# First 512 tokens as one block, masks of the second batch on VectorE, and exponentials that wait at a table change

## The chip, the cores and the metric

The kernel runs on one core of one Trainium2 chip. The metric is the device time of one execution in microseconds; the time before is the median of three runs. A profiled execution of the same program, whose rows are read below, has a span (first to last instruction) and a time of its own. TensorE appears in the rows as PE (matrix products) and PEld (loads of the stationary operand), VectorE as DVE, ScalarE as ACT, GpSimd as POOL, SyncE as SP.

## The reference

Four batches of 576 tokens go through an attention of 8 heads of 64 columns, then through two feed-forward layers (512 to 2048 to 512). In heads 0 to 3 a token sees itself and the 31 tokens before it ("local"), in heads 4 to 7 every 32nd token before it ("strided").

```python
scores = scale * np.matmul(q, k.transpose(0, 1, 3, 2))
masks = np.stack([mask_local if h < H // 2 else mask_strided for h in range(H)], axis=0)
scores = np.where(masks[None, :, :, :], scores, -1000000000.0)
...
attn = attn / (np.sum(attn, axis=-1, keepdims=True) + 1e-09)
return np.matmul(attn, v).astype(np.float32)
# x: the 2304 tokens of attn_out, 512 columns
h = x @ w_in;  g = h * np.tanh(softplus(h));  x = g @ w_out      # first layer ("moe")
h = x @ w_in;  g = h - np.tanh(h);            return g @ w_out   # second layer ("moe2")
```

The weights of both layers arrive as 64-bit floats.

## The kernel before

**A planner writes the order.** Every piece of work is a task (class `Plan`, `add`) with a cost for each engine that can do it, a key, the tasks that it follows and the buffers that it takes and frees. While the program is built, `Plan.run` goes through the tasks by modelled time: of all waiting tasks it takes the one that can start first, and of equals the one with the smaller key, and so fixes the order of the instructions on each engine. Keys come from a list of due times (`due`), which walks over the steps below at modelled TensorE costs (`pe_cost`), with `ATTEND` added for a step that runs beside attention. A function of another table on ScalarE (`EXPS` for exp and ln, `MISH`, `TANH`) costs a table load (L193), modelled as `SWITCH`, and its key is raised by `PATIENCE`. `fill` (L479) puts small matrix products on TensorE into gaps that the planner sees early in the program.

**Attention** is done in 16 pairs of heads (`pair`), four for each batch, two strided and then two local, and each pair in two halves (`half_pair`): scores (L589), row maxima, exponentials (L634 or L645), normalisation, transposes on TensorE (L697), their copies (L449, L451), the products with v (L715), and the copy of the result to `xr`. The first batch (`BY_PE`) leaves the division to the end: the totals are summed on TensorE (L731) and ScalarE inverts them (L735, L738), VectorE multiplies (L749). In batches listed in `LEAN`, the first two, TensorE adds the mask to the scores by a bf16 product with an identity (L586), VectorE reduces to the maxima (L617), and ScalarE reads the scores out of PSUM, whose banks it frees; ScalarE may also normalise (L665). In the others VectorE adds the mask, takes the maximum and writes the masked scores to SBUF in one instruction per unit (`masked_max`, L622), which frees the banks at once.

**The first layer** runs over blocks of tokens and 16 chunks of 128 hidden columns. A step (`step`) is one chunk of one block: 12 products (`gemm1`, L855: four pieces of 128 input columns, each with high part by high, low by high, and high by low part), then on ScalarE the activation (L874), its split into parts (L449 or L451, and L455), and two steps later (`LAG`) 12 products of `gemm2` (L906). Before, the blocks are 256, 256, 512, 384, 512 and 384 tokens wide, and the first two are run against each other: five steps of the first, then one of each in turn, so that a new chunk of weights is needed every second step. Both take their x straight from the attention of the first batch (`x_split`); two local pairs (`LATE`) load and compute their second halves later, since the first block needs only tokens 0 to 255. Later blocks load x from DRAM (`x_load`). Two sets of x tiles (`TB`, 512 and 384 wide) alternate between blocks.

**Weights** (`weights`): each of the 32 half chunks is loaded, shrunk (L402 or L405), turned to fp32 by three VectorE instructions (L414, L419, L424), and split (a cast on ScalarE or VectorE, a subtraction on VectorE).

**The second layer** (`unit`, `factors`) runs over 512, 512, 512, 512 and 256 tokens with a scheme of seven products instead of eight; its weights are made from 64-bit floats (`keep_in`, `keep_out`) while the last blocks of the first layer run.

Of the kernel before, what the change touches and what calls it, by code (L numbers as in the profile page):

```python
# [56 lines left out]
class Plan:  # L57
# [15 lines left out]
    def add(self, engs, fn, key, after=(), take=(), give=(), dma=None, start=0.0, rows=128, table=None, bulk=False):  # L73
# [9 lines left out]
        return t  # L83

    WINDOW = 3.4133
    warm, window, busy, heat, table = False, 0, 0.0, 0.0, None
# [44 lines left out]
    def run(self):  # L131
# [14 lines left out]
        while left:  # L146
# [5 lines left out]
            for e, q in waiting.items():  # L152
                for t in q:
                    start = self.room(t, max(engines[e], t.ready, now))
                    if start == INF:
                        continue
                    key, end = t.key, start + t.engs[e]
                    if e == ACT and t.table not in (None, self.table):
                        key += self.PATIENCE
                        end += self.SWITCH  # L160
                    if best is not None and (start, key) >= best[:2]:
                        continue
                    if any(
                        u.key + HOLD < t.key and start < u.ready < end - 0.05
                        and end - u.ready > HOLDW * (u.ready - start) and self.room(u, u.ready) < end
                        and all(max(engines[o], u.ready) + c > u.ready + HOLDO for o, c in u.engs.items() if o != e)
                        for u in q
                    ):
# [49 lines left out]
def pe_cost(n):  # L218
    return {256: 0.12, 384: 0.174, 512: 0.227}.get(n, 0.0004375 * n + 0.007)
# [23 lines left out]
def attention_two_moe(  # L243
# [17 lines left out]
    scale = 1.0 / float(D) ** 0.5  # L261
    blocks = [[256, 256, 512, 384, 512, 384], [512] * 4 + [256]]
    TB = (512, 384)
# [13 lines left out]

    pieces2 = [(0, starts[0][2])] + list(zip(starts[0], blocks[0]))[2:]
    x2d = {
# [68 lines left out]

    steps = [(0, 0, c) for c in range(HEAD)]
    for c in range(NC):  # L350
        steps += [(0, 1, c)] + ([(0, 0, c + HEAD)] if c + HEAD < NC else [])
    steps += [(0, j, c) for j in range(2, len(blocks[0])) for c in range(NC)]
    NU, HALF = NC // 2, 256
# [4 lines left out]
    for l, j, c in steps:  # L358
        if l == 0 and j == 0:
            t_ = max(t_, FIRST + PACE * c)  # L360
        due.append(t_)
        if l == 0:
            t_ += 24 * pe_cost(blocks[l][j]) + (ATTEND if 1 < j < 5 else 0.0)
        else:
            t_ += (42 if blocks[1][j] > HALF else 24) * pe_cost(HALF) + 6 * blocks[1][j] // 128 * pe_cost(DM)
    due += [t_, t_ + 4, t_ + 8, t_ + 12]
    first_use = [min(step_of[0, j, c] for j in range(2)) for c in range(NC)]

# [119 lines left out]

    BY_PE, LEAN = (0,), (0, 1)
    ON_ACT = [(0, 0), (0, 1), (1, 0), (1, 1)]  # L490

    def pair(i):
# [274 lines left out]

        inner = starts[0][2]
        x_slot = ["xr0", "wi9", "wo9", "wi8"][i] if first else "xr0"
        xb = Buf([x_slot], 5) if first else Buf([x_slot], 1)  # L770
        done = [half_pair(0), half_pair(1)]
        plan.link(*done)
        cols = slice(inner, S) if first else slice(0, S)
        if first:
            for j in range(2):
                t0, n = starts[0][j], blocks[0][j]
                x_split(0, j, p, [done[0]] if i in LATE and j == 0 else done,
                        lambda t0=t0, n=n: st["x"][:, t0:t0 + n], xb,
                        k0 + 3 if j == 0 else due[step_of[0, 1, 0]] - 3)
            free_first[x_slot] = [split[j][p][1] for j in range(2)]  # L780
            for n, what in enumerate("qkv"):
                free_first[slot_of_first(i, what)] = last_s[i] if what != "v" else last_pv
# [28 lines left out]
    def x_load(l, j, p, key):  # L811
# [18 lines left out]

        after = [x_store[p, c[0]] if l == 0 else x2_store[p, 0, c[0] + 1] for c in cut]
        J = len(blocks[0]) * l + j
        x = add({SP: 0.45 * len(cut)}, load, key - 5, after + [last_g1[J - 2]], take=[buf], dma=0.7)
        x_split(l, j, p, [x], lambda: h["t"], buf, key)
# [6 lines left out]
    def step(s):  # L841
# [50 lines left out]
        m = KC  # L892

        both = J < 2
        wide = starts[0][2] if both else n
        cols = slice(starts[0][J], starts[0][J] + n) if both else slice(0, wide)
        opens, closes = c == 0 and J != 1, c == NC - 1 and J != 0
        k2 = due[s + LAG] + 0.1
        for f in range(m):
# [16 lines left out]
            if closes:  # L916
# [9 lines left out]
                def store(e, f=f):  # L926
                    nc.sync.dma_start(out=x2d[f, j - 1], in_=t_ev[J, f])

# [191 lines left out]
    def factors(j, key, ready):  # L1120
# [5 lines left out]
        def load_of(x):  # L1126
# [15 lines left out]

            after = [x2_store[2 * lower + k, 0, i[0] + 1] for k in range(2) for i in cut] + old
            return add({SP: 0.9 * len(cut)}, load, key - 5 + len(raw_loads), after, take=[buf], dma=0.7), buf

        def tiles():
# [8 lines left out]
            hi = [one_(t[:, 2 * i:2 * i + 2]) for t in (a, b) for i in range(m)]  # L1155
            if J % 2 == 0:
                lo = [hi.pop()] + [one_(sb([128, 2, HALF], F32R, slot, "xq")) for slot in ("q0", "q1", "k0", "k1")]
                t = sb([128, 4, HALF], F32R, "v", "xq")
                lo += [one_(t[:, :2]), one_(t[:, 2:])]
            else:  # L1160
                hi += [one_(sb([128, 2, HALF], F32R, "xr0", "xq"))]
                t = sb([128, 9, HALF], F32R, "pp", "xq")
                lo = [one_(t[:, 2 * i:2 * i + 2]) for i in range(4)]
                lo += [one_(cols(W2[u, 3][:, 1, :])) for u in (2 * NS, 2 * NS + 1)]
                lo += [two_(*(sb([128, 1, HALF], F32R, f"pT{i}", "xq") for i in range(2)))]
            xq[J] = list(zip(hi, lo))
# [248 lines left out]
    with tc.manual_schedule():  # L1415
# [8 lines left out]
        for c in range(NC):  # L1424
            for half in "io":
# [9 lines left out]
                weights(0, half, c, free_first.get(tag, []), due_w - 3.514, kd)  # L1435
        for s in range(2 * NC):
# [40 lines left out]
        order = [(i, g) for i in range(len(pairs)) for g in range(2)]  # L1477
        x, y = LATE
        order[2 * x:2 * x + 4] = [(x, 0), (y, 0), (x, 1), (y, 1)]
        for a, b in zip(order, order[1:]):  # L1480
# [56 lines left out]
```

## Time and profile before

| | |
|---|---|
| median of three runs | 892.72 us (891.67 to 892.78) |
| profiled execution | 891.31 us, span 889.5 us |
| TensorE products busy | 882.3 us (99% of the span), 6080 instructions |
| VectorE busy | 593.0 us (67%) |
| ScalarE busy | 429.3 us (48%), 89.8 us of it in 70 table loads |
| granted TensorE clock, mean | 0.999 |

A product on TensorE is shown longer than the distance to the next one, because products overlap; what one costs in a stream is read from start to start, or from the merged pieces of the chain of work. The same holds for the instructions of VectorE and ScalarE, less strongly. Idle time in square brackets stands behind the instruction that it precedes, with what ended it.

### The profile page before, as it was taken

To read this page: it belongs to the slowest core of one execution; us is meant where nothing else is said; L and a number is where in the kernel's file an instruction comes from. 1 tells how busy PE (TensorE), PEld (TensorE's weight loads), DVE (VectorE), ACT (ScalarE), POOL (GpSimd) and SP (SyncE) were. 2 spreads that over 40 slices of the span, in tenths; PEclk is the share of its full clock that TensorE was granted. 3 is DMA by queue.
4 is the path that set the end of the run, shared out by engine and by line. 5 is a ranking of instruction groups with operands and counts; after the bars stand their busy time and mean duration, and the time that the engine had idled before them with its cause. 6 is when DMAs were issued, how large, how long until landed. Compare 5 with 4: busy or idle time off the path is not lost.

```text
span 889.5 us, 16480 instructions
## 1 busy us (share of the span) xinstructions
PE 882.3 (99%) x6080; PEld 788.3 (89%) x6080; DVE 593.0 (67%) x1578; ACT 429.3 (48%) x910; POOL 2.4 (0%) x13
## 2 busy tenths in 40 slices
PE   8999999999999999999999999999999999999998
PEld 7899999877778999888999999898999889998896
DVE  6999998556565657778776885575457545555533
ACT  7999999656446625443444532252224222322211
POOL 1000000000000000000000000000000000000000
PEclk9999999999999999999999999999999999999999
DMA  9981113411112149877787443352235223655531
GB/s 308 379 340 55 59 59 102 150 62 33 63 66 91 43 149 317 253 260 258 252 282 233 133 152 102 112 190 95 96 132 176 95 96 119 209 169 162 175 125 62
DMA packets 84657, 138.19 MB, mean 155 GB/s; under 512 B 10016, under 2 KB 37152, under 8 KB 84576
## 3 DMA queue, kind: packets, MB, share of 16 engines
q1 hardware_dynamic: 84576, 137.14, 46.1%
q8 instruction: 48, 0.79, 0.4%
q14 instruction: 33, 0.27, 0.1%
HBM read 107.22 MB, written 29.88 MB: 154 GB/s over the span
## 4 chain that ended last, share of the span: by engine, by line
PE 93%; ACT 4%; DVE 1%; DMA 1%; issue 0%; SPq 0%; ACTq 0%
PE acc L1382 22%; PE h L855 22%; PE acc L906 22%; PE hx L1245 18%; PE hx L1262 3%; PE sps L589 2%; PE ops L715 2%; PE ptps L697 2%; ACT p L645 1%; DMA kT<-in_k_dram 1%; ACT stwo L402 0%; ACT pT L449 0%; ACT L193 0%; ACT stwi L402 0%; ACT dd L735 0%
## 5 line engine op out<-in xcount | busy, mean ns | idle before, releaser
L855 PE MATMUL h<-xh,wi 128*128 128x256 f32 (+2 forms) x768 | 215.1, 342 | 0.6 <-ACT B L874 0.5
L906 PE MATMUL acc<-gh,wo 128*128 128x256 f32 (+2 forms) x768 | 196.5, 341 | 0.0
L1382 PE MATMUL acc<-w,gh 128*128 128x512 f32 x576 | 179.1, 392 | 0.0
L1245 PE MATMUL hx<-xq,w 128*128 128x256 f32 x1280 | 174.1, 284 | 0.0
L1245 PEld LDWEIGHTS hx<-xq,w 128*128 128x128 f32 x1280 | 167.6, 191 | 6.5
L855 PEld LDWEIGHTS h<-xh,wi 128*128 128x128 f32 x768 | 137.9, 189 | 14.4 <-ACT B L874 1.0
L906 PEld LDWEIGHTS acc<-gh,wo 128*128 128x128 f32 x768 | 132.1, 189 | 10.4
L855 PE MATMUL h<-xl,wi 128*128 128x256 f32 (+2 forms) x384 | 129.4, 337 | 0.1
L906 PE MATMUL acc<-gl,wo 128*128 128x256 f32 (+2 forms) x384 | 128.9, 336 | 0.0
L1382 PEld LDWEIGHTS acc<-w,gh 128*128 128x128 f32 x576 | 103.2, 188 | 18.1 <-DVE gh L451 0.4
L1382 PE MATMUL acc<-w,gl 128*128 128x512 f32 x288 | 112.2, 389 | 0.0
L1333 ACT ACTIVATE th<-hx 128x256 f32<-128x256 f32 x48 | 18.5, 385 | 160.2 <-PE hx L1245 120.1
L193 ACT ACT_TABLE_LOAD x70 | 89.8, 1283 | 1.2
L874 ACT ACTIVATE B<-h 128x256 f32<-128x256 f32 (+2 forms) x96 | 46.9, 492 | 89.5 <-PE h L855 87.0
L1338 DVE SCALAR_TENSOR_TENSOR H<-hx,th 128x256 f32<-128x256 f32 x48 | 20.3, 423 | 98.7 <-ACT th L1333 98.6
L455 DVE TENSOR_TENSOR gl<-B,gh 128x256 fp32r<-128x256 f32 (+2 forms) x96 | 52.9, 553 | 46.6 <-ACT gh L449 44.1
L1333 ACT ACTIVATE th<-H 128x256 f32<-128x256 f32 x64 | 33.5, 524 | 95.2 <-PE acc L1382 51.0
L455 DVE TENSOR_TENSOR H<-H,hx 128x256 f32<-128x256 f32 x160 | 66.9, 418 | 17.3 <-PE hx L1245 8.4
L906 PEld LDWEIGHTS acc<-gl,wo 128*128 128x128 f32 x384 | 72.5, 189 | 5.1
L855 PEld LDWEIGHTS h<-xl,wi 128*128 128x128 f32 x384 | 72.5, 189 | 5.0 <-DVE xl L455 0.3
L1382 PEld LDWEIGHTS acc<-w,gl 128*128 128x128 f32 x288 | 54.1, 188 | 12.1 <-DVE gl L455 0.2
L1338 DVE SCALAR_TENSOR_TENSOR H<-H,th 128x256 f32<-128x256 f32 x64 | 35.7, 558 | 40.2 <-ACT th L1333 39.9
(118 smaller groups left out, 1020.7 us busy)
## 6 DMA issues: line engine op xcount, KB each, us to landing
w<-w2o SPq DMA_DIRECT2D x160, 256.0 KB, 2.6
stwi<-in_moe_w_in_dram SPq DMA_DIRECT2D x16, 512.0 KB, 7.7
stwo<-in_moe_w_out_dram SPq DMA_DIRECT2D x16, 512.0 KB, 8.9
w2v<-in_moe_w_out_dram SPq DMA_DIRECT2D x32, 256.0 KB, 4.0
w2o<-p SPq DMA_DIRECT2D x48, 128.0 KB, 3.4
w<-w2i SPq DMA_DIRECT2D x24, 256.0 KB, 3.0
out_dram<-ev SPq DMA_DIRECT2D x18, 256.0 KB, 3.7
w2v<-in_moe_w_in_dram SPq DMA_DIRECT2D x8, 512.0 KB, 3.9
```

Source lines behind the costliest of these rows:

```text
L193: self.load_table(t.table)
L455: eng.tensor_tensor(out=out, in0=a, in1=b, op=op)
L589: nc.tensor.matmul(s[a][:, at_, :], tq[64 * a:64 * a + 64, q0:q0 + nq], tk[64 * a:64 * a + 64, k0_:k0_ + nk], start=not lean, stop=not lea ...
L697: nc.tensor.transpose(t[:, n, :], h["p", a][:, n, :], ident[:nq, :nq])
L855: nc.tensor.matmul(h_ps[s], w[:, wp, kc, :], xx[:, kc, :n], start=(kc == first_kc and i == 0), stop=(kc == last_kc and i == 2),)
L874: nc.scalar.activation(out=b_tile(), in_=h_ps[s], func=ACTF.Mish, scale=2.0 ** -8)
L906: nc.tensor.matmul(acc[f][:, cols], w[:, wp, 128 * f:128 * f + 128], g, start=(opens and i == 0), stop=(closes and i == 2),)
L1245: nc.tensor.matmul(st[t], w[:, wp, 256 * i + 128 * k:256 * i + 128 * k + 128], unit_of(xq[J][x][xp], k)[:, 0], start=(q in (1, 6, 7, 5) an ...
L1262: nc.tensor.matmul(st[t], w[:, wp], unit_of(xq[J][kc // 2][xp], kc % 2)[:, 0], start=(kc == 0 and m == 0), stop=(kc == KC - 1 and m == 2),)
L1333: nc.scalar.activation(out=st["th", i][:, cols], in_=x, func=ACTF.Tanh, scale=2.0 ** -8)
L1338: nc.vector.scalar_tensor_tensor(out=st["H", i][:, cols], in0=x, scalar=2.0 ** -8, in1=st["th", i][:, cols], op0=ALU.mult, op1=ALU.subtract,)
L1382: nc.tensor.matmul(acc[f], g[:, 128 * f:128 * f + 128], where[wp](), start=(opens and m == 0), stop=(closes and m == 2),)
```

## The change

The first two blocks become one of 512 tokens, and the widths are 512, 384, 512, 384, 512; no pair is late, all four pairs of the first batch are loaded and computed whole before the first step ends. The tiles of the second layer's x swap their places to follow the new count of blocks. `LEAN` loses the second batch: its masks and maxima are those of the third and fourth, and its normalisation is VectorE's alone. In the planner a task of the exp table that needs a table load may start no earlier than 6.0 us after it became ready; tasks of the table that is loaded are free of this.

```diff
+    DWELL = {EXPS: 6.0}
...
                     if e == ACT and t.table not in (None, self.table):
                         key += self.PATIENCE
-                        end += self.SWITCH
+
+                        start = max(start, t.ready + self.DWELL.get(t.table, 0.0))
+                        end = start + t.engs[e] + self.SWITCH
...
-    blocks = [[256, 256, 512, 384, 512, 384], [512] * 4 + [256]]
+    blocks = [[512, 384, 512, 384, 512], [512] * 4 + [256]]
...
-    steps = [(0, 0, c) for c in range(HEAD)]
-    for c in range(NC):
-        steps += [(0, 1, c)] + ([(0, 0, c + HEAD)] if c + HEAD < NC else [])
-    steps += [(0, j, c) for j in range(2, len(blocks[0])) for c in range(NC)]
+    steps = [(0, j, c) for j in range(len(blocks[0])) for c in range(NC)]
...
-            t_ += 24 * pe_cost(blocks[l][j]) + (ATTEND if 1 < j < 5 else 0.0)
+            t_ += 24 * pe_cost(blocks[l][j]) + (ATTEND if j < 4 else 0.0)
...
-        since = max(x_due[b - 1], due[step_of[0, 1, 0]])
+        since = max(x_due[b - 1], due[step_of[0, 0, 1]])
...
-    LATE = (2, 3)
-    pass
+    LATE = ()
...
-    BY_PE, LEAN = (0,), (0, 1)
+    BY_PE, LEAN = (0,), (0,)
...
         if first:
-            for j in range(2):
-                t0, n = starts[0][j], blocks[0][j]
-                x_split(0, j, p, [done[0]] if i in LATE and j == 0 else done,
-                        lambda t0=t0, n=n: st["x"][:, t0:t0 + n], xb,
-                        k0 + 3 if j == 0 else due[step_of[0, 1, 0]] - 3)
+            n = blocks[0][0]
+            x_split(0, 0, p, done, lambda: st["x"][:, :n], xb, k0 + 3)
...
-            if J % 2 == 0:
-                lo = [hi.pop()] + [one_(sb([128, 2, HALF], F32R, slot, "xq")) for slot in ("q0", "q1", "k0", "k1")]
+            if J % 2 == 1:
+                lo = [one_(sb([128, 2, HALF], F32R, slot, "xq")) for slot in ("q0", "q1", "k0", "k1", "xr0")]
...
-        for J in range(2, last + 1):
-            if J < 2 + B - 1:
-                for i in range(KC * (J - 1), KC * J):
+        for J in range(1, last + 1):
+            if J < B:
+                for i in range(KC * J, KC * J + KC):
                     pair(i)
```

## Rows read from the trace of the kernel before

**Rows 1.** Busy time by engine in three stretches; PEclk is the granted clock.
```profile
38.48:60.00 21.52, 20.99 (x198) 18.88 (x197) 21.48 (x52) 21.39 (x50) 0.00 (x0) 1.00 1.02 399
60.00:155.00 95.00, 94.96 (x949) 89.06 (x949) 89.39 (x282) 92.39 (x231) 0.00 (x0) 1.00 0.25 78
155.00:320.00 165.00, 165.00 (x1124) 137.53 (x1119) 96.69 (x390) 92.66 (x133) 0.00 (x0) 1.00 0.23 74
```

**Rows 2.** Order of time on PE, 30 to 157 us: start, length, work.
```profile
30.12 0.36 PE L855 MATMUL h<-xh,wi 128*128 128x256 f32 x1
...
32.89 0.39 PE L855 MATMUL h<-xl,wi 128*128 128x256 f32 x1
...
38.36 0.28 PE L855 MATMUL h<-xh,wi 128*128 128x256 f32 x1
...
43.88 0.71 PE L731 MATMUL tot<-pT,ones 128*64 128x288 f32 x4
...
45.14 0.47 PE L697 MATMUL ptps<-ident,p 96*128 96x96 f32 x3
...
58.67 0.38 PE L855 MATMUL h<-xh,wi 128*128 128x256 f32 x1 [0.53 <-ACT B L874]
...
156.59 0.48 PE L855 MATMUL h<-xh,wi 128*128 128x512 f32 x1
```

**Rows 3.** Chain that ended last, merged pieces: start, length, work.
```profile
85.75 1.44 PE h L855 x12
...
355.47 2.72 PE acc L906 x12
...
501.86 5.08 PE hx L1245 x42
```

**Rows 4.** Order of time on PE around scores, with and without mask products.
```profile
52.80 0.41 PE L586 MATMUL sps<-mstrb,identb 72*72 72x288 bf16 x2
53.14 0.74 PE L589 MATMUL sps<-kT,qT 64*72 64x72 f32 x16
...
93.88 0.49 PE L586 MATMUL sps<-mfirst,identb 96*96 96x384 bf16 x2
94.30 0.90 PE L589 MATMUL sps<-kT,qT 64*96 64x128 f32 x12
...
274.40 0.39 PE L906 MATMUL acc<-gl,wo 128*128 128x512 f32 x1
274.72 0.90 PE L589 MATMUL sps<-kT,qT 64*96 64x128 f32 x12
```

**Rows 5.** Order of time on DVE: results of the first batch's half pairs.
```profile
13.97 0.68 DVE L749 TENSOR_TENSOR xr<-ops,dd 128x288 f32<-128x288 f32 x1 [0.53 <-ACT dd L738]
...
30.86 0.44 DVE L749 TENSOR_TENSOR xr<-ops,dd 128x288 f32<-128x288 f32 x1
...
46.40 0.45 DVE L749 TENSOR_TENSOR xr<-ops,dd 128x288 f32<-128x288 f32 x1
...
52.39 0.45 DVE L749 TENSOR_TENSOR xr<-ops,dd 128x288 f32<-128x288 f32 x1
```

**Rows 6.** Order of time on DVE: maxima with TensorE's mask, then with VectorE's.
```profile
63.43 0.81 DVE L617 TENSOR_REDUCE rows<-sps 72x4 f32<-72x288 f32 x2
...
134.25 0.23 DVE L622 CUSTOM_DVE_ANT_0 p<-sps,mstr 72x72 f32<-72x72 f32 x1 [0.42 <-PE sps L589]
...
135.47 0.45 DVE L455 TENSOR_TENSOR p<-p,rows 72x288 f32<-72x288 f32 x1
```

**Rows 7.** Groups on ACT, 36 to 150 us: count, busy us, mean ns.
```profile
L193 ACT ACT_TABLE_LOAD x34 | 43.6, 1283 | 0.6
...
L665 ACT ACTIVATE p<-p,rows 96x128 f32<-96x128 f32 x12 | 3.8, 398 | 0.0
L665 ACT ACTIVATE p<-p,rows 72x72 f32<-72x72 f32 x8 | 2.2, 355 | 0.0
```

**Rows 8.** Order of time on ACT: last result of the second batch.
```profile
138.53 0.39 ACT L449 ACTIVATE xr<-ops 128x288 f32<-128x288 f32 x1
```

More of the change, by code (lines that the diff above doesn't have):

```diff
@@ L276, in attention_two_moe @@
     starts = [[sum(bl[:j]) for j in range(len(bl))] for bl in blocks]
-    pieces2 = [(0, starts[0][2])] + list(zip(starts[0], blocks[0]))[2:]
+    pieces2 = list(zip(starts[0], blocks[0]))
     x2d = {
@@ L366, in attention_two_moe @@
     due += [t_, t_ + 4, t_ + 8, t_ + 12]
-    first_use = [min(step_of[0, j, c] for j in range(2)) for c in range(NC)]
+    first_use = [step_of[0, 0, c] for c in range(NC)]
     def block_of(token):
@@ L766, in pair @@
         last_pv = []
-        inner = starts[0][2]
+        inner = starts[0][1]
         x_slot = ["xr0", "wi9", "wo9", "wi8"][i] if first else "xr0"
-        xb = Buf([x_slot], 5) if first else Buf([x_slot], 1)
+        xb = Buf([x_slot], 3) if first else Buf([x_slot], 1)
         done = [half_pair(0), half_pair(1)]
@@ L774, in pair @@
         if first:
-            for j in range(2):
-                t0, n = starts[0][j], blocks[0][j]
-                x_split(0, j, p, [done[0]] if i in LATE and j == 0 else done,
-                        lambda t0=t0, n=n: st["x"][:, t0:t0 + n], xb,
-                        k0 + 3 if j == 0 else due[step_of[0, 1, 0]] - 3)
-            free_first[x_slot] = [split[j][p][1] for j in range(2)]
-            for n, what in enumerate("qkv"):
+            n = blocks[0][0]
+            x_split(0, 0, p, done, lambda: st["x"][:, :n], xb, k0 + 3)
+            free_first[x_slot] = [split[0][p][1]]
+            for n_, what in enumerate("qkv"):
                 free_first[slot_of_first(i, what)] = last_s[i] if what != "v" else last_pv
@@ L829, in load @@
                 nc.sync.dma_start(out=t[:, lo - t0:hi - t0], in_=src[:, lo - a:hi - a])
-        after = [x_store[p, c[0]] if l == 0 else x2_store[p, 0, c[0] + 1] for c in cut]
+        after = [x_store[p, c[0]] if l == 0 else x2_store[p, 0, c[0]] for c in cut]
         J = len(blocks[0]) * l + j
-        x = add({SP: 0.45 * len(cut)}, load, key - 5, after + [last_g1[J - 2]], take=[buf], dma=0.7)
+        x = add({SP: 0.45 * len(cut)}, load, key - 5, after + [last_g1.get(J - 2)], take=[buf], dma=0.7)
         x_split(l, j, p, [x], lambda: h["t"], buf, key)
@@ L892, in step @@
         m = KC
[L894 to L897, printed above, removed]
+        wide, cols = n, slice(0, n)
+        opens, closes = c == 0, c == NC - 1
         k2 = due[s + LAG] + 0.1
@@ L926, in store @@
                 def store(e, f=f):
-                    nc.sync.dma_start(out=x2d[f, j - 1], in_=t_ev[J, f])
+                    nc.sync.dma_start(out=x2d[f, j], in_=t_ev[J, f])
                 ev = add({ACT: act_cost(wide, True), DVE: dve_cost(wide)}, evac, k2 - 8, [x], take=[eb], give=[ab])
@@ L1141, in load @@
                         nc.sync.dma_start(out=t[:, k, lo - a0:hi - a0], in_=x2d[2 * lower + k, i][:, lo - a:hi - a])
-            after = [x2_store[2 * lower + k, 0, i[0] + 1] for k in range(2) for i in cut] + old
+            after = [x2_store[2 * lower + k, 0, i[0]] for k in range(2) for i in cut] + old
             return add({SP: 0.9 * len(cut)}, load, key - 5 + len(raw_loads), after, take=[buf], dma=0.7), buf
@@ L1155, in tiles @@
             hi = [one_(t[:, 2 * i:2 * i + 2]) for t in (a, b) for i in range(m)]
-            if J % 2 == 0:
-                lo = [hi.pop()] + [one_(sb([128, 2, HALF], F32R, slot, "xq")) for slot in ("q0", "q1", "k0", "k1")]
+            if J % 2 == 1:
+                lo = [one_(sb([128, 2, HALF], F32R, slot, "xq")) for slot in ("q0", "q1", "k0", "k1", "xr0")]
                 t = sb([128, 4, HALF], F32R, "v", "xq")
                 lo += [one_(t[:, :2]), one_(t[:, 2:])]
+                hi += [two_(*(sb([128, 1, HALF], F32R, f"pT{i}", "xq") for i in range(2)))]
             else:
-                hi += [one_(sb([128, 2, HALF], F32R, "xr0", "xq"))]
+                lo = [hi.pop()]
                 t = sb([128, 9, HALF], F32R, "pp", "xq")
-                lo = [one_(t[:, 2 * i:2 * i + 2]) for i in range(4)]
+                lo += [one_(t[:, 2 * i:2 * i + 2]) for i in range(4)]
                 lo += [one_(cols(W2[u, 3][:, 1, :])) for u in (2 * NS, 2 * NS + 1)]
-                lo += [two_(*(sb([128, 1, HALF], F32R, f"pT{i}", "xq") for i in range(2)))]
             xq[J] = list(zip(hi, lo))
@@ L1435, in attention_two_moe @@
                 weights(0, half, c, free_first.get(tag, []), due_w - 3.514, kd)
-        for s in range(2 * NC):
+        for s in range(NC):
             step(s)
         last = len(blocks[0]) - 1
-        for J in range(2, last + 1):
-            if J < 2 + B - 1:
-                for i in range(KC * (J - 1), KC * J):
+        for J in range(1, last + 1):
+            if J < B:
+                for i in range(KC * J, KC * J + KC):
                     pair(i)
@@ L1477, in attention_two_moe @@
         order = [(i, g) for i in range(len(pairs)) for g in range(2)]
-        x, y = LATE
-        order[2 * x:2 * x + 4] = [(x, 0), (y, 0), (x, 1), (y, 1)]
         for a, b in zip(order, order[1:]):
```

## The prediction

> **What bounds the kernel now.** I read the busy time by stretches first. From 60 to 155 us TensorE is busy for 94.96 of 95.00 us, from 155 to 320 for all of it, at the full granted clock [rows 1]; the page's total (99%) says the same of the rest. So after the start the end is set by the work that TensorE has to do, and a change is worth what it takes from that work, plus what it does to the moment at which TensorE starts to be fed. The second view is TensorE in order of time near 30 to 60 us: the first step begins at 30.12 in pieces, and from 38.48, 0.12 behind the last row of that start, the stream is closed but for one wait of 0.53 us on an activation [rows 2]. The third is the chain of work, from which I take what a product costs in a stream [rows 3]. VectorE and ScalarE come last: they are nearly full as well from 38 to 155 us (89.39 and 92.39 of 95) and far from it later (97 and 93 of 165) [rows 1]. They are hidden, but in the stage that the change rebuilds the cover is thin.
>
> **Wider first block.** Before, 2 blocks x 16 steps x 24 = 768 products of 256 columns: 12 take 1.44 us, 0.120 each, so 92.2 us. After, 384 of 512 columns: 12 take 2.72 us, 0.2267 each, so 87.0 us [rows 3]. That is **-5.1 us**, the largest term. The 256-column price is no effect of the crowded stage: at 501.86 us, in the second layer, 42 products of 256 columns take 5.08 us, 0.121 each [rows 3]. The Trainium skill (TensorE: Matmul & The Clock Gate, section Back-to-back issue gap) gives an isolated warm product N/2.4 + 2.5 ns. As an estimate by that page, halving the count would save 384 x 2.5 ns, about 1.0 us; the rows differ from it, and they are of this kernel. The same widths follow in another order; the rest of the layer's products are unchanged.
>
> **Masks off TensorE.** A half pair of the second batch loses two bf16 products. Their distance to the first score is 53.14 - 52.80 = 0.34 us when strided and 94.30 - 93.88 = 0.42 when local [rows 4]; four of each make 3.0 us, the upper bound. But where scores follow a layer's product with no mask between, there is a hole: 274.40 + 0.227 = 274.63, and the scores start at 274.72 [rows 4], 0.09 us that the mask covered. I take that off eight times: **-2.3 us**.
>
> **The start.** All eight half pairs of the first batch must now be done before the first step can go past its first quarter. Six results came between 13.97 and 30.86 us, one per 3.4 us [rows 5]. Two more at this pace bring the eighth to 37.6. In the trace the product that needs the low part of the sixth's x starts at 32.89, 2.0 us after its result's start [rows 2, 5]; with 512 columns to split I use that. TensorE is fed for good from 39.6 us, instead of 38.48. What it has behind it by then differs: before, 30 products of 256 (first at 30.12, last at 38.36) [rows 2], 3.6 us; after, three of 512, 0.7. And before, 4.1 us of the first batch's attention were still to come: the last scores with their mask (0.42 + 0.83), twice totals and products with v (45.14 - 43.88 = 1.26 each) and transposes (about 0.3) [rows 2, 4]; after, none. Sum: 39.6 - 38.48 + 3.6 - 0.7 - 4.1 = -0.1. Between results 3.0 and 3.9 us apart the term is -0.9 to +0.9. I take **-0.1**. The chunks are no hurdle there: a new chunk is due every 24 x 0.2267 = 5.4 us instead of 2.9 for the first five.
>
> **Work for VectorE and ScalarE.** Eight masked units take 135.47 - 134.25 = 1.22 us, two reductions 0.81 [rows 6]: 0.41 more per half pair, 3.3 us for eight taking the strided price for all. Twenty ScalarE instructions normalise six tiles now [rows 7] (three a local, four a strided tile); on VectorE each takes about 0.45 [rows 6]: 2.7 more. Fewer, wider splits give about 1.4 back (two of 256 columns against one of 512). So VectorE has some 4.6 us more to do, and the stage is 7.5 us shorter, against 95 - 89.39 = 5.6 us idle [rows 1]. I still price it at nothing: in that stage VectorE also starts on the third batch (the masked units at 134.25 are its), which can wait until after 155 us, where 40% of VectorE is idle, and it does casts and copies that ScalarE can take.
>
> **Waiting exponentials.** ScalarE loads tables 34 times from 36 to 150 us, 43.6 us [rows 7], nearly half its time. If exponentials gather for 6 us, I expect some 16 to 22 loads there and 40 to 55 in all instead of 70. No load is TensorE's wait, but for the 0.53 us, so this is worth at most **0.5 us**, which I leave out against small new waits; it frees 15 to 20 us of ScalarE and so pays for the cover above. What it delays: each half pair by up to 6 us, and behind it transposes and products with v. The clock I take as it is: the gaps of the start are filled with small products as before.
>
> **Sum.** -5.1 - 2.3 - 0.1 = -7.5 us. The profiled execution (span 889.5) had 891.31, 1.4 below the median of 892.72. Span after: 882.0; profiled time 883.8; median **885.2**. With the bounds together (-5.1 - 3.0 - 0.9 - 0.5, and -5.1 - 2.3 + 0.9) 883.2 to 886.2; since the planner writes every order anew, I call 882.2 to 888.2 this case: 0.64.
>
> **Rivals.** (1) *The start is later.* Halves seven and eight of the trace came 52.39 - 46.40 = 6.0 us apart [rows 5], when weights shared both engines. If that is the pace, TensorE is fed 2 x 2.6 = 5.2 us later: 890.4. Against it: they had low keys there, and now they have the same high keys as the first six. 0.13.
> (2) *The width saves little*, since the 13 ns by which a 256-column product exceeds half a 512 one go with weight loads and their neighbours: only the masks and the start are left, -2.4 us: 890.3. The second layer's row at 501.86 speaks against it [rows 3]. 0.04. The page of the Trainium skill cited above would have it nearly so, with 1.0 us kept.
> (3) *VectorE becomes the bound.* If ScalarE isn't relieved and the third batch can't wait (its tokens are needed from 896 instead of 1024 on, a quarter of a block sooner), VectorE lacks 4.6 + 7.5 - 5.6 = 6.5 us, which TensorE waits out: 891.7. 0.06.
> (4) *Slower: the waiting exponentials make the second batch late for the second block.* Its first scores are at 52.80 and its last result at 138.53 [rows 4, 8], 10.7 us per half pair; the first step that needs it starts at 156.59 [rows 2], 18 us later. With two half pairs in flight, w us of waiting each add up to 8w / 2, at 6 us 24. The stage gets 7.5 us shorter, so 10.5 of the lead are left: TensorE waits from w = 2.6 on, the kernel is slower from w = 4.5 on, and at 6 us it is -7.5 + 13.5 = +6.0: 898.7. Against it: at 10.7 us a half pair the pace is the planner's choice and not the chain's, and the second batch's keys now begin after the first step instead of the fifth, some 15 us earlier by the list of due times. 0.07.
> (5) *The wait does nothing*: loads stay near 70. As ScalarE is off the path, the time is that of the forecast, and it is no case of its own. The remaining 0.06 is for what I don't see, half on each side.
>
> **Numbers.** 0.2% (1.8 us) is about what a measurement of this kernel can tell from no change. Forecast, rivals 1 and 2 and half the rest are faster: 0.84. Same: rival 3 and a little, 0.08. Slower: rival 4 and a little, 0.08. The range 882.0 to 890.5 holds the forecast and rivals 1 and 2, some 0.81.
>
> **What would show it.** Right: 1152 products of 512 columns in L855 and L906 and none of 256, at 2.72 us per 12; L586 with 16 instructions, not 32; the first step's second quarter at 38 to 41 us and no gap on TensorE above 0.5 us after it; table loads well under 70; VectorE above 95% until about 145 us and the first 384-column step at 147 to 150. Wrong: the stream closing at 43 us or later; waits of TensorE on weights (VectorE) or on x of the second block; 512-column products dearer than 0.23 us beside attention.

## The result, and the profile after

The changed kernel has a median of **883.66 us** over 20 executions, the kernel before, beside it on the same chip, 892.41: ratio 0.9912, 95% interval 0.9886 to 0.9938. The forecast was 885.2, with a range of 882.0 to 890.5. In 5 of the 20 executions the mean granted clock was 0.984 to 0.987 instead of 1.0 and the time 891.3 to 894.1; the ratio takes these in (the two medians alone stand at 0.9902), the first profile is one of them, and "the profile after" is therefore that of the first experiment below, the same kernel at 884.06 us with a span of 882.3, against 891.31 and 889.5 before.

Busy time by stretches (as in [rows 1]: start and end, length, then busy us and instructions of PE, PEld, DVE, ACT, POOL, then PEclk, DMA share, GB/s):

```profile
38.48:60.00 21.52, 21.49 (x185) 17.23 (x183) 21.30 (x78) 19.29 (x50) 0.00 (x0) 1.00 1.00 391
60.00:155.00 95.00, 94.69 (x610) 73.35 (x611) 90.85 (x315) 75.38 (x177) 0.00 (x0) 1.00 0.27 90
155.00:320.00 165.00, 165.00 (x1134) 141.85 (x1133) 96.57 (x385) 75.49 (x125) 0.00 (x0) 1.00 0.24 77
```

TensorE stays full. VectorE has a little more to do from 60 to 155 us than before, ScalarE 17 us less (75.38 against 92.39).

Groups of TensorE by shape (count, busy us, mean ns):

```profile
L851 PE MATMUL h<-xh,wi 128*128 128x512 f32 x384 | 132.0, 399 | 0.0
L899 PE MATMUL acc<-gh,wo 128*128 128x512 f32 x384 | 120.4, 394 | 0.0
...
L851 PE MATMUL h<-xl,wi 128*128 128x512 f32 x192 | 75.1, 391 | 0.0
L899 PE MATMUL acc<-gl,wo 128*128 128x512 f32 x192 | 75.0, 391 | 0.0
...
L478 PE MATMUL fill<-ones 128*128 128x128 bf16 x155 | 12.6, 252 | 1.0 <-DVE ones L1412 1.0
...
L585 PE MATMUL sps<-mfirst,identb 96*96 96x384 bf16 x8 | 2.0, 326 | 0.0
L585 PE MATMUL sps<-mstrb,identb 72*72 72x288 bf16 x8 | 1.7, 293 | 0.0
```

These are the 1152 products of 512 columns that were forecast; no group of 256 columns is left in L851 and L899 (L855 and L906 before). The mask products are 16 instead of 32, the filling products 155, where the kernel before has 176.

The chain of work, merged pieces (start, length, work), answering to [rows 3]:

```profile
68.89 2.72 PE h L851 x12
71.61 2.72 PE acc L899 x12
...
120.26 0.68 DVE gl L455
...
127.42 0.60 DVE wo L455
...
132.91 0.47 PE ptps L696 x3
```

Twelve products of 512 columns cost 2.72 us beside attention too, as taken. From 120.26 to 132.91 the chain runs over VectorE: the cover was used up, though not overdrawn, for TensorE's idle time in all of 60 to 155 us is 0.31 us, the wait for VectorE's maxima that ends at 132.91.

The start, in order of time on TensorE (answers to [rows 2]):

```profile
1.00 6.13 PE L478 MATMUL fill<-ones 128*128 128x128 bf16 x57 [1.00 <-DVE ones L1412]
...
32.47 0.74 PE L588 MATMUL sps<-kT,qT 64*72 64x72 f32 x16
...
35.88 0.50 PE L851 MATMUL h<-xh,wi 128*128 128x512 f32 x1
...
39.57 0.74 PE L588 MATMUL sps<-kT,qT 64*72 64x72 f32 x16
40.25 1.29 PE L478 MATMUL fill<-ones 128*128 128x128 bf16 x20
41.35 0.48 PE L851 MATMUL h<-xh,wi 128*128 128x512 f32 x1
```

In the kernel before the first line reads:

```profile
1.00 4.79 PE L479 MATMUL fill<-ones 128*128 128x128 bf16 x57 [1.00 <-DVE ones L1419]
```

The first and the last two results of the first batch, in order of time on VectorE (answers to [rows 5]):

```profile
15.15 0.68 DVE L748 TENSOR_TENSOR xr<-ops,dd 128x288 f32<-128x288 f32 x1 [0.90 <-ACT dd L737]
...
36.10 0.45 DVE L748 TENSOR_TENSOR xr<-ops,dd 128x288 f32<-128x288 f32 x1
...
38.95 0.45 DVE L748 TENSOR_TENSOR xr<-ops,dd 128x288 f32<-128x288 f32 x1
```

The second quarter of the first step starts at 41.35 (forecast 39.6, with 38 to 41 as the sign of being right). Scores of the second batch already stand in front of it, at 32.47 and 39.57. The first step of 384 columns starts at 144.27; the forecast was 147 to 150. Groups on ScalarE, table loads in the whole span:

```profile
L196 ACT ACT_TABLE_LOAD x38 | 48.8, 1283 | 0.6
```

38 loads instead of 70; 16 of them from 36 to 150 us, where [rows 7] have 34.

### The profile page after: what moved, and what is told of

Its sections match the earlier page's. It is cut to its first block, busy times and chain, and to the rows that moved or that the text cites. A ratio compares the mean times of both kernels' runs of the same rounds, so it can differ in the third digit from the quotient of the medians.

```text
span 891.9 us, 15576 instructions
## 1 busy us (share of the span) xinstructions
PE 884.7 (99%) x5659; PEld 771.4 (86%) x5659; DVE 588.3 (66%) x1633; ACT 391.6 (44%) x851; POOL 2.4 (0%) x13
## 4 chain that ended last, share of the span: by engine, by line
PE 95%; DVE 2%; DMA 1%; ACT 1%; issue 0%; SPq 0%; DVEq 0%
PE acc L1375 22%; PE h L851 22%; PE acc L899 21%; PE hx L1238 18%; PE sps L588 3%; PE hx L1255 3%; PE ops L714 2%; PE ptps L696 2%; DMA kT<-in_k_dram 1%; PE tot L730 1%; PE fill L478 1%; DVE wcv L424 0%; DVE wcv L419 0%; PE sps L585 0%; DVE wo L455 0%
## 5 line engine op out<-in xcount | busy, mean ns | idle before, releaser
L851 PE MATMUL h<-xh,wi 128*128 128x512 f32 (+1 forms) x640 | 207.2, 377 | 0.0
L899 PE MATMUL acc<-gh,wo 128*128 128x512 f32 (+1 forms) x640 | 186.4, 372 | 0.0
L851 PEld LDWEIGHTS h<-xh,wi 128*128 128x128 f32 x640 | 119.1, 188 | 17.0 <-ACT B L870 0.2
L899 PEld LDWEIGHTS acc<-gh,wo 128*128 128x128 f32 x640 | 116.4, 188 | 15.1
L851 PE MATMUL h<-xl,wi 128*128 128x512 f32 (+1 forms) x320 | 117.9, 368 | 0.0
L899 PE MATMUL acc<-gl,wo 128*128 128x512 f32 (+1 forms) x320 | 117.8, 368 | 0.0
L870 ACT ACTIVATE B<-h 128x512 f32<-128x512 f32 (+1 forms) x80 | 44.5, 556 | 117.9 <-PE h L851 113.7
L455 DVE TENSOR_TENSOR gl<-B,gh 128x512 fp32r<-128x512 f32 (+1 forms) x80 | 50.8, 635 | 41.7 <-ACT gh L449 39.6
L899 PEld LDWEIGHTS acc<-gl,wo 128*128 128x128 f32 x320 | 60.1, 188 | 7.7
L851 PEld LDWEIGHTS h<-xl,wi 128*128 128x128 f32 x320 | 60.2, 188 | 6.4
L455 DVE TENSOR_TENSOR gl<-H,gh 128x512 fp32r<-128x512 f32 (+1 forms) x80 | 51.1, 639 | 7.5 <-ACT gh L449 4.5
```

What stands on the lines that cost most here:

```text
L455: eng.tensor_tensor(out=out, in0=a, in1=b, op=op)
L851: nc.tensor.matmul(h_ps[s], w[:, wp, kc, :], xx[:, kc, :n], start=(kc == first_kc and i == 0), stop=(kc == last_kc and i == 2),)
L870: nc.scalar.activation(out=b_tile(), in_=h_ps[s], func=ACTF.Mish, scale=2.0 ** -8)
L899: nc.tensor.matmul(acc[f][:, cols], w[:, wp, 128 * f:128 * f + 128], g, start=(opens and i == 0), stop=(closes and i == 2),)
```

## Experiments

The theory to be tested is that of the forecast: TensorE is the bound, the wider block and the masks each take their part off it and add up, and the wait of the exponentials is worth nothing. Rivals: the parts do not add (VectorE has room for the masks only if the block is wide); the wait holds up the second batch; the width saves little. A to H in the expectations are explained there; two more letters, further down, are theories on the clock: J, that TensorE's wait for keys near 8 to 10 us lets the granted clock fall, and K, that the thin stretch of 10 to 28 us does so by itself. Kernels of one group ran on one chip beside the kernel before.

**The changed kernel again**, unchanged.

> The changed kernel as it is. In 15 of its 20 executions it took 882.5 to 884.1 us at a granted clock of 0.999 to 1.000, in 5 of them 891.3 to 894.1 at 0.984 to 0.987; the profile that was kept is one of the five. Theory A (the gain is TensorE work: widths -5.1, masks -2.3, start about 0): undisturbed executions at 883 to 884.5 again, 0.990 to 0.992 of the kernel before, and in an undisturbed profile a span of 881 to 882.5 with the first step's second quarter at 38 to 41 us. Rival B (the start is earlier or later than I reckoned, and the width or mask term is off to match): the same time, but a second quarter outside 38 to 41 us.

883.45 us (12 executions), ratio 0.9929 [0.9897, 0.9962]; four of the 12 at 891.8 to 893.6. Its profile is shown above: the span of 882.3 is the expected one, the second quarter at 41.35 lies 0.35 us outside the expected 38 to 41. So, by the letter, it is rival B that came: the time is right and the terms are not quite.

**Without the wait.**

```diff
-    DWELL = {EXPS: 6.0}
+    DWELL = {}
```

> The changed kernel without the 6 us wait of exponentials. Theory A: ScalarE is off the path, so the wait is worth at most 0.5 us: 883 to 885 undisturbed, and some 65 to 75 table loads instead of the changed kernel's count. Rival C (the wait pays for the cover: without it ScalarE and VectorE are short in the first block and TensorE waits): 886 us or more, with waits of TensorE on weights or x between 45 and 150 us.

883.07 us, ratio 0.9906 [0.9870, 0.9941]; 58 table loads instead of 38 (65 to 75 were expected). The wait saves 20 loads, 26 us of ScalarE, and no time: within this change it is worth 0 to what can be measured.

**Masks of the second batch back on TensorE**, wait kept.

```diff
-    BY_PE, LEAN = (0,), (0,)
+    BY_PE, LEAN = (0,), (0, 1)
```

> The changed kernel with the second batch's masks, and its right to normalise on ScalarE, given back. Theory A: +2.3 us (3.0 at most), 885.5 to 887 undisturbed, with 16 more mask products. Rival D (VectorE has no room in that stage, so taking 5 us off it repays the 2.3): no change, 883 to 884.5. Rival E (scores that wait in PSUM for exponentials hold the banks, so giving the masks back costs more than the products): 888 or more.

895.16 us, ratio 1.0043 [1.0013, 1.0073], as rival E has it: 11.7 us more than with the masks on VectorE, five times the mask term. TensorE in order of time, the second batch's local scores and what follows:

```profile
102.27 0.90 PE L588 MATMUL sps<-kT,qT 64*96 64x128 f32 x12
...
117.42 0.90 PE L588 MATMUL sps<-kT,qT 64*96 64x128 f32 x12
...
132.50 0.90 PE L588 MATMUL sps<-kT,qT 64*96 64x128 f32 x12
...
156.49 2.24 PE L478 MATMUL fill<-ones 128*128 128x128 bf16 x37
...
163.45 0.42 PE L851 MATMUL h<-xh,wi 128*128 128x384 f32 x1
```

The scores are 15.1 us apart, the last at 132.50 (at 107.21 in the profile after, the line below), and the second block's x is late: 138 filling products from 140 to 165 us, 9.56 us.

```profile
107.21 0.90 PE L588 MATMUL sps<-kT,qT 64*96 64x128 f32 x12
```

What holds a half pair up stands in the order of time of all engines, behind the scores of 117.42:

```profile
118.35 1.02 DVE L616 TENSOR_REDUCE rows<-sps 96x3 f32<-96x384 f32 x2
...
123.96 1.28 ACT L196 ACT_TABLE_LOAD   x1
...
125.25 0.36 ACT L644 ACTIVATE p<-sps,rows 96x128 f32<-96x128 f32 x1
```

The maxima are done at 119.37, the table load for the exponentials starts at 123.96. Here `p` is made from `sps`: the scores hold their PSUM banks through the wait, and the half pair's exponentials and transposes are all behind it when the next scores come at 132.50. With the masks on VectorE the exponentials read `p` (L644 `p<-p,rows`, 56 in the group view of the profile after), and the banks are free behind the maxima. That it is the banks that tie the half pairs together is read from this order and the code, not tried by itself; the same edit also lets ScalarE normalise again, and the two are not separated. Rival 4 of the prediction is at work here, but only with the masks on TensorE.

**The same with a wait of 2.0 us** instead of 6.0.

```diff
-    DWELL = {EXPS: 6.0}
+    DWELL = {EXPS: 2.0}
```

> The changed kernel with the second batch's masks on TensorE again, and the waiting of the exponentials shortened from 6.0 to 2.0 us. With 6.0 us the scores of the second batch's local half pairs came 15.1 us apart (102.27, 117.42, 132.50) and its x was late for the second block: 895.16; without the wait 888.26. If each half pair waits once, in its turn, because its masked scores hold the PSUM banks until the exponentials have run, the distance is 15.1 - 4.0 = 11.1 us, the second batch ends some 4 half pairs x 4.0 = 16 us sooner or more, which is about the length of the stretch with filling products (144 to 163 us), and the kernel is at 888 to 890, without filling products after 60 us. If the wait does its harm in another way (fewer table loads, other order), the time stays near 895 or lies in the middle, and the distance doesn't follow the wait.

886.9 us, ratio 0.9931 [0.9898, 0.9965], below the 888 to 890 expected; no filling product behind the start. From the second batch's first scores to its last: 85.0 us without the wait (the blocks alone, below: 32.42 to 117.41), 88.1 with 2.0 us (41.35 to 129.43, in an execution with a late start), 100.5 with 6.0 (32.02 to 132.50), 74.7 with 6.0 and the masks on VectorE (32.47 to 107.21). So the starving goes with the wait, but not by its full length for every half pair: 2 us cost 3 us over seven distances and not 14; slack that the planner had in them would explain it, but isn't shown. The expected 11.1 us between scores was missed (14.1, 10.4 and 13.4). Each against the kernel before beside it, this version gains 5.4 us and the one without a wait, below, 4.1: a short wait does not harm even here.

**Old blocks, with the masks on VectorE and the wait.** The kernel before with

```diff
+    DWELL = {EXPS: 6.0}
...
-                        end += self.SWITCH
+                        start = max(start, t.ready + self.DWELL.get(t.table, 0.0))
+                        end = start + t.engs[e] + self.SWITCH
...
-    BY_PE, LEAN = (0,), (0, 1)
+    BY_PE, LEAN = (0,), (0,)
```

> The kernel before with the other two parts alone: masks of the second batch on VectorE and waiting exponentials, blocks of 256, 256, 512, 384, 512 and 384. Theory A: only the mask term is left, -2.3 us to the kernel before, 889.5 to 891. Rival F (with two narrow blocks the cover is too thin for either part, and the three parts help only together): 892 or more.

893.83 us, ratio 1.0008 [0.9991, 1.0024]: no gain, as rival F has it. The gain that the masks should have brought stands as filling products: 235, 59 more than before, 59 of them from 50 to 80 us, where the kernel before has none; they come ahead of the late local pairs' totals and of the products behind them.

**The blocks alone**: the changed kernel with the masks on TensorE and no wait.

```diff
-    DWELL = {EXPS: 6.0}
+    DWELL = {}
-    BY_PE, LEAN = (0,), (0,)
+    BY_PE, LEAN = (0,), (0, 1)
```

> The changed blocks alone: masks of the second batch on TensorE, no waiting exponentials. Giving the masks back to TensorE cost 11.7 us where exponentials wait, and the extra is 156 small filling products on TensorE, most of them at 146 to 163 us: x of the second block came late. Theory G (scores that wait in PSUM for a waiting exponential hold the two banks, so the second batch's chain stretches; the wait and the masks belong together): without the wait no filling after 50 us, and the plain price of the mask products, 885.5 to 887 undisturbed. Rival H (the masks alone, by the banks that are held until the exponentials are done, stretch the chain in any case): 890 or more, with filling at 140 to 165 us.

888.26 us, ratio 0.9937 [0.9909, 0.9965], so -4.1 between the medians (892.38 before), between what G and H expected. The interval (-8.1 to -3.1) holds the -5.2 of the prediction's terms for width and start, but it is that wide because the clock had fallen in 5 of the 30 executions beside it and in none of these. Where it was above 0.998 the medians differ by 4.0 us, with a standard deviation of 0.4 and 0.6 us, so 1.2 us of the 5.2 are missing. No filling products after 50 us.

**The masks alone**: the kernel before with

```diff
-    BY_PE, LEAN = (0,), (0, 1)
+    BY_PE, LEAN = (0,), (0,)
```

> The kernel before with the second batch's masks on VectorE alone: old blocks, no wait. With the wait as well it came out 1.7 us above the kernel before instead of 2.3 below, with 59 more filling products, at 50 to 65 us. Theory G2 (the wait delays the late halves of the first batch, which the second narrow block needs; the masks by themselves are worth 2.3): 889.5 to 891, without filling at 50 to 65 us. Rival F (VectorE has no room for the masks beside two narrow blocks): 892 or more.

894.75 us, ratio 1.0019 [0.9985, 1.0053]: +2.4 where -2.3 stands in the prediction; the interval (-1.3 to +4.7) excludes -2.3. This is rival F again; filling products at 50 to 65 us are gone, as G2 expected, but others stand later. In order of time on TensorE:

```profile
87.59 1.46 PE L479 MATMUL fill<-ones 128*128 128x128 bf16 x23
88.86 0.48 PE L906 MATMUL acc<-gh,wo 128*128 128x256 f32 x2
```

And on VectorE at the same time:

```profile
85.54 0.66 DVE L419 SCALAR_TENSOR_TENSOR wcv<-stwi,wcv 128x512 int32<-128x512 int32 x1
86.12 0.45 DVE L455 TENSOR_TENSOR p<-p,rows 72x288 f32<-72x288 f32 x1
86.49 0.68 DVE L419 SCALAR_TENSOR_TENSOR wcv<-stwo,wcv 128x512 int32<-128x512 int32 x1
87.09 0.68 DVE L424 SCALAR_TENSOR_TENSOR wcv<-stwi,wcv 128x512 int32<-128x512 int32 x1
87.69 0.41 DVE L455 TENSOR_TENSOR gl<-B,gh 128x256 fp32r<-128x256 f32 x1
88.03 0.68 DVE L455 TENSOR_TENSOR wo<-wcv,wo 128x512 fp32r<-128x512 f32 x1
```

TensorE fills from 87.59 and takes up L906 at 88.86, right behind the low part of `wo` that VectorE makes from 88.03 to 88.71, in a row of instructions without a gap. VectorE has 92.87 of 95 us in 60 to 155 (before 89.39). Filling products from 80 to 140 us take 3.24 us in all, in three places, the waits of TensorE on ScalarE's `B` (1.3) and on the maxima (0.3) are 1.1 more than before, the saved masks 2.3: +2.0 by rows, +2.4 measured. So TensorE does wait beside the old blocks, as rival 3 has it, and VectorE is the cause in the place shown (1.3 us). What the other two places (111.61 and 113.50) wait for was not followed, and 1.3 us are waits on ScalarE.

**Filling products ahead of the third keys.** The first profile of the changed kernel shows what happens where the clock falls. Busy time and granted clock (PEclk, third column from the end):

```profile
0.00:10.00 10.00, 7.01 (x95) 6.13 (x95) 3.45 (x15) 3.65 (x13) 2.42 (x13) 1.00 0.79 216
10.00:20.00 10.00, 9.92 (x98) 8.26 (x100) 5.53 (x16) 6.37 (x27) 0.00 (x0) 0.53 1.07 353
20.00:35.00 15.00, 15.00 (x128) 12.25 (x126) 10.40 (x26) 10.18 (x31) 0.00 (x0) 0.50 0.78 301
35.00:40.00 5.00, 5.00 (x58) 3.91 (x56) 3.27 (x9) 3.69 (x12) 0.00 (x0) 0.70 0.92 319
40.00:60.00 20.00, 19.57 (x220) 15.86 (x221) 19.72 (x76) 19.23 (x56) 0.00 (x0) 1.00 0.81 297
```

The same execution in order of time on TensorE:

```profile
10.08 0.78 PE L588 MATMUL sps<-kT,qT 64*72 64x72 f32 x16 [2.07 <-DMA kT<-in_k_dram]
...
36.82 1.17 PE L714 MATMUL ops<-pT,vl 128*64 128x96 f32 x12
37.92 0.71 PE L696 MATMUL ptps<-ident,p 96*128 96x96 f32 x6
38.47 1.50 PE L478 MATMUL fill<-ones 128*128 128x128 bf16 x24
...
45.90 0.50 PE L851 MATMUL h<-xh,wi 128*128 128x512 f32 x1
```

TensorE waits 2.07 us for k, and from then to 38 us the granted clock is 0.50, the level of 1.2 GHz, although TensorE is busy 15.00 of 15.00 us from 20 to 35; the first step comes at 45.90 instead of 35.88. The same scores in three other profiles, in this order: without the wait of the exponentials, with one of 2.0 us and the masks on TensorE, and with one of 6.0 us and the masks on TensorE:

```profile
9.54 0.74 PE L588 MATMUL sps<-kT,qT 64*72 64x72 f32 x16 [1.61 <-DMA kT<-in_k_dram]
10.17 0.74 PE L588 MATMUL sps<-kT,qT 64*72 64x72 f32 x16 [1.66 <-DMA kT<-in_k_dram]
9.11 0.74 PE L588 MATMUL sps<-kT,qT 64*72 64x72 f32 x16 [1.08 <-DMA kT<-in_k_dram]
```

In the first two the clock fell to 0.50 within 2 us, in the third it stayed. It also stayed in the kernel before, with a wait of 0.66 us (the same scores, at 8.77), and in every other profile with a wait of 0.32 us or none, the profile after among them; one more, with later keys, is told below. The test puts 28 filling products in front of those scores:

```diff
+    GUARD = 28
...
+                if i == 1 and g == 0:
+                    slot = next(x for x in plan.fill_slots if plan.free.get(x, 0.0) <= plan.engines[PE])
+                    for _ in range(GUARD):
+                        fill(slot)
+                    plan.free[slot] = plan.engines[PE] + 3.0
```

> The changed kernel with 28 filling products (some 1.5 us) on TensorE ahead of the scores of the second pair, where two of the slower profiles show a wait of 1.6 and 2.1 us for k. Theory J (that wait drops the clock in some executions; the small products of the attention then run at the lower clock up to 38 us or more): hardly any execution at a granted clock of 0.98, all at 882.5 to 885. Rival K (the thin stretch of TensorE between 10 and 28 us drops it, four filling products there against 28 before): a quarter of the executions still at 891 to 894.

884.96 us, 7 executions from 884.56 to 885.5, ratio 0.9902 [0.9865, 0.9939], none with the clock fallen (882.5 to 885 was expected of all):

```profile
8.31 1.73 PE L478 MATMUL fill<-ones 128*128 128x128 bf16 x28
9.97 0.74 PE L594 MATMUL sps<-kT,qT 64*72 64x72 f32 x16
```

The products fill 8.31 to 9.97 and the scores follow without a wait.

**With 12 of them.**

```diff
-    GUARD = 28
+    GUARD = 12
```

> The changed kernel with 12 filling products (instead of 28) ahead of the scores that can wait for the third transfer of keys. 12 of them at the 0.06 us of the full clock are 0.7 us, less than the 2.07 us that TensorE waited in the profiled execution with the clock dropped. Theory J (the wait for k at 8 to 10 us lets the granted clock fall) expects a wait of up to 1.3 us to be left in some executions: a median of 883.5 to 884.5 and still some executions at 891 to 894, but fewer than one in four. Theory K (the thin stretch from 10 to 28 us drops it by itself) expects one in four as before.

885.15 us, ratio 0.9920 [0.9884, 0.9956]; 2 of 12 executions at 894.8 and 897.1, fewer than one in four; the median is above the 883.5 to 884.5 expected. In its profile a wait of 0.32 us for k is left and the clock holds. That the wait was longer in the two is likely, but no profile shows it.

**28 of them and no wait of the exponentials.**

```diff
-    DWELL = {EXPS: 6.0}
+    DWELL = {}
```

> The changed kernel with 28 filling products ahead of the third transfer's scores and with the waiting of the exponentials taken out. Theory J expects what the same 28 gave with the wait: none of the executions above 887, median 884 to 885.5. Theory K expects one in four at 891 to 894. That the waiting matters for the start is the rival: then this one lies over 1 us from 884.96.

885.41 us (884.91 to 885.83, 4 executions), ratio 0.9911 [0.9876, 0.9945]. No fall, and the wait has no part in it.

**28 of them in the kernel before**, by the same edit.

> The kernel before with the same 28 filling products ahead of the third transfer's scores. About one in five of its executions so far lay 5 to 10 us above the rest, at a granted clock of 0.985 to 0.988. Theory J (it is the wait for k at 8 to 10 us, in either kernel) expects these to be gone and the median within +0 to +1.5 us of the kernel before. Theory K, or that the dropped executions have nothing to do with the change's start, expects them to stay at about one in five.

895.97 us, ratio 1.0018 [0.9988, 1.0048], 11 executions from 894.94 to 898.53. None with the clock fallen (beside it 6 of 23 of the kernel before, at 900.1 to 901.6), but the price is 3.5 us, more than the 1.5 expected.

**The third keys issued later**, behind three other transfers.

```diff
-                    {SP: 0.45}, lambda e, w=w: load_qk(w, None), k0 - 20 + n if not first else -200 + 3 * i + n,
+                    {SP: 0.45}, lambda e, w=w: load_qk(w, None), k0 - 20 + n if not first else -200 + 3 * i + n + (3.5 if i == 1 and w == "k" else 0),
```

> The changed kernel with the load of that k issued three loads later, so that TensorE waits for it longer in every execution. Theory J: half of the executions or more at a granted clock of 0.98 and 891 to 896 us. Rival K: a quarter, as in the changed kernel, and the others some 1 to 2 us slower for the later start.

889.52 us, ratio 0.9937 [0.9909, 0.9966]: six of 10 executions at 889.5 to 889.8 with a mean clock of 0.994, four at 885.7 to 886.5 with 1.0. The planner knew of the late keys and filled the gap itself, and the clock fell later, to 0.68 in 20 to 30 us and 0.81 in 30 to 40. There is no wait for keys in this profile; before the fall, near 23.8, TensorE was busy for 4.83 of the 6 us from 18 to 24, with waits on ScalarE:

```profile
21.31 0.71 PE L730 MATMUL tot<-pT,ones 72*64 72x144 f32 x8 [0.53 <-ACT pT L449]
...
23.20 0.90 PE L696 MATMUL ptps<-ident,p 72*72 72x72 f32 x8 [0.64 <-ACT dd L734]
```

So the wait for keys is not the only thing behind which it fell: a thin stretch did it here, as K said. Neither theory's numbers came (J: half of the executions at 891 to 896; K: a quarter).

## Why the prediction was right, and where not

**The forecast's case came**: -8.8 us between the medians, -7.2 between the two profiled executions, -7.5 forecast. That the sum came so near is in part luck: the blocks alone gave 1.1 us less than their two terms (-4.1 for -5.2), and the masks beside them 2.9 more than theirs (-5.2 for -2.3).

*Width, -5.1.* The count and the 2.72 us per 12 are as predicted; the blocks alone gave -4.1. Of the 1.1 that are missing the start holds a part, since there, with the masks of the second batch on TensorE, the second quarter begins at 43.16: by the reckoning of the next paragraph (2.5 us of the second batch done by then, the first result 0.8 us late) that start is +0.2 instead of -0.1. Some 0.8 stays open, and nothing shows whether it belongs to the width. Rival 2 would have left the blocks alone at the start's -0.1, outside the interval of -8.1 to -3.1. By the gap that the Trainium skill gives (TensorE: Matmul & The Clock Gate, Back-to-back issue gap) they would have been, as an estimate, at -1.1, outside it too; the rows of 0.120 and 0.2267 us decide. The 13 ns of rival 2 are the gain of a pair of products: one of 256 columns exceeds half a 512 one by 6.7 ns (0.120 - 0.1133).

*The start, -0.1.* In the profile after: 41.35 - 38.48, plus 3.6, less 0.7 and 4.1 as in the prediction, less 1.34 for the two scores of the second batch that were already done: +0.3. But the first 57 filling products, which the change does not touch, took 6.13 us in that execution and 4.79 in the one before, and the first result came at 15.15 instead of 13.97 [rows 5], 1.2 us later. In the 14 profiles these 57 products took 4.60 to 6.13 us, and 4.68 in another execution of the changed kernel, so the reason is scatter between executions and not the change. Without it the term is -0.9, the lower bound, and the difference of the profiles -8.4, against -5.1 - 2.3 - 0.9 = -8.3 by the terms and -8.8 by the medians. The second quarter's 41.35, 0.35 outside the sign of 38 to 41, is 40.2 without it. The eighth result was forecast for 37.6 and came at 38.95, 37.8 without the 1.2. Rival 1, six microseconds between the last halves, did not come: 38.95 - 36.10 = 2.85.

*Masks, -2.3.* The term was mis-sized, and it is not a term by itself. Beside the wide block the masks are worth 888.26 - 883.07 = 5.2 us (both without the wait, from two groups of runs); beside the narrow blocks they cost 2.4. What was left out on the gain's side: with the masks on TensorE the eighth result of the first batch is at 40.05 instead of 38.95 and there are 18 more filling products in the start, some 1.1 us. The rest, about 1.8, is not settled. It seems to go with the missing wait: with the masks on TensorE and 2.0 us of it the kernel lies 3.4 us above the changed one (886.9 and 883.45, two groups of runs), and that is 2.3 + 1.1. On the cost's side the prediction put the work for VectorE at nothing, as the third batch could wait and ScalarE would help. In the whole change that held, and a part of the reason was under-priced: from 38.48 to 320 us the masks bring VectorE 208.7 - 202.4 = 6.3 us (changed kernel against the blocks alone; forecast 6.0), and the wide block takes 207.6 - 202.4 = 5.1 from it (forecast 1.4, the splits alone). The net is +1.2 instead of +4.6. Part of the 5.1 is work that ScalarE took over, as the blocks alone bring the table loads from 70 to 58. These sums hold for this window: over the whole span VectorE is busy for 587.3 us with the masks, 583.9 with the blocks alone and 593.0 before, because the planner also moves casts and copies between engines and times.

*Waiting exponentials, 0.* Right: 883.45 with and 883.07 without. The loads, 38, are below the 40 to 55 expected, and 16 from 36 to 150 us are within the 16 to 22. With the masks on TensorE the wait is not worth nothing: 2.0 us gain some 1.3, 6.0 cost 6.9. Rival 4 was refused for a reason that is not the one that decides. The prediction argued from the lead of 18 us and the planner's pace; the runs show that a wait of 6 us does starve TensorE (+6.9 us, 895.16 against 888.26) where the exponentials read the scores from PSUM, and not where VectorE has moved them to SBUF. The mask change is what makes the wait harmless; that it does so by the banks is the likely reading.

*What would show it.* VectorE at 95.6% from 60 to 155 us, no gap of TensorE above 0.5 us behind the start: as said. The second quarter came 0.35 us after the window given for it, the first 384-column step 3 us before the early end of its window.

*The clock.* "The clock I take as it is" was right for the median and wrong as a statement on the start: 9 of 32 executions of the changed kernel lost 8 to 10 us to it (3 of 12 without the wait of the exponentials; the kernel before 21 of 105 beside these experiments). With 28 filling products it was 0 of 22 in three kernels; three kernels without them had 0 of 12, 0 of 10 and 1 of 10 as well. The waits of 1.61 to 2.07 us in all three profiles with an early fall, against 1.08 or less in those without, support the wait for k as the cause, but it is not proven for every execution, and the fall with later keys came without it.

## What to carry to other kernels

Two changes to one stage that share an engine's spare time are not two terms: price each with and without the other, for here the masks gave 5.2 us beside a wide block and cost 2.4 beside narrow ones. Before an instruction is made to wait, ask what its operands hold meanwhile; here the wait did harm only while they stood in PSUM. Where the program fills known gaps, count the filling products as idle time: TensorE showed 94.4 of 95 us busy in the kernel that lost 11.7.

Of the versions tried none beats the changed kernel by its median, as the 883.07 without the wait is within the scatter. By the mean over executions the one with 28 filling products is 0.7 us ahead, 884.99 (7 executions) against 885.72 (20), as it trades 1.5 us in each for the fallen clock in some; with so few executions that is no proof.

## What the runs showed of the hardware

One wait of 2.07 us at 8 to 10 us was followed by some 27 us at a granted clock of 0.50, the level of 1.2 GHz. All through it TensorE is shown busy, 15.00 of 15.00 us from 20 to 35, with the small products of attention. The clock rose to 1.00 near 37.9 us, where the transposes of 37.92 run at their full pace (0.71 us for six, against 1.22 at 32.48). It rose before the next filling product (38.47) and the first wide one (45.90), so neither brought it back. The three other profiles with a fallen clock agree: it rose near 37.8, 35.6 and 33.8 us, and the next filling products came at 37.98, 37.01 and 34.37.

The Trainium skill (TensorE: Matmul & The Clock Gate, What's actually happening) says that the lower level is the default and activity releases it. The first filling products agree: in the kernel before, 8 of them fall into 3.5 to 4.0 us and 13 into 4.5 to 5.0, though the granted clock reads 1.00 in both. That a stream which the profile shows as full stayed at the lower level for so long is what this trace adds; why it did, no run here tells.
